# Decode attention with a large KV cache: K transposed as fp32 words, scores in two passes, and PV that streams V four tiles wide

## The chip, the cores and the metric

The kernel runs on one core of one Trainium2 chip. The metric is the device time of one execution in microseconds (us). A ratio is always the mean time of one kernel's fast runs over that of the other's fast runs of the same rounds on the same chip, so it is not quite the ratio of the medians that are quoted beside it.

The span of a profile is about 1.8 us shorter than the time of the same run; all instants below count from the span's first instruction.

## The reference

One token attends to 32,768 cached positions: 8 KV heads ("groups") with 4 query heads each, head size 128. A small SwiGLU feed-forward runs beside it, and a sigmoid gate mixes the two.

```python
def _A_ref(x, k_cache, v_cache, wq, wo):          # k_cache, v_cache: [1, 8, 32768, 128] bf16
    q = (x @ wq) as [1, 32, 1, 128]
    scores = einsum("bhqd,bhkd->bhqk", q, k) * Dh ** -0.5
    p = softmax(scores)
    o = einsum("bhqk,bhkd->bhqd", p, v)
    return o.reshape(1, 1, 4096) @ wo              # wo: [4096, 512]
# _B_ref: (silu(x @ w_gate) * (x @ w_up)) @ w_down
# result: g * a + (1 - g) * b, g = sigmoid(sum(x * gate_w))
```

K and V are 134 MB of the 148 MB that the kernel reads. Each byte is used once.

## The kernel before

One queue (SP) streams everything in a fixed order into a ring of five 4 MB slots: wq, halves of K and V (16,384 positions each), the feed-forward weights, and wo last. A slot is loaded again when PE has released it. The last half of V and wo are cut into four loads each, so that PE can follow them.

```python
RH = S // 256          # 128 tiles of 128 positions in one half
TPF = 8                # tiles per "fill"
V_LAST = (64, 32, 16, 16); WO_CUT = (16, 8, 4, 4)
stream = [("wq",), ("K", 0, 0), ("F1",), ("K", 0, 1), ("F2",)]
for g in range(1, G):
    for hf in range(2):
        stream += [("K", g, hf), ("V", g - 1, hf)]
stream += [("V", G - 1, 0), ("V", G - 1, 1), ("wo",)]
# ... SP: for each entry wait for the slot's release (five entries back), then dma_start
```

PE transposes K eight tiles at a time, DVE copies the transposed tiles out of PSUM, and PE multiplies them with the queries. ACT takes the exponential. PV uses each V tile as weights and streams four columns of probabilities through it.

```python
def emit_fill(j, src, q):
    if j >= NST:
        pe.wait_ge(sem_cp, j - NST + 1)
    stb = pst[j % NST]
    for t in range(TPF):
        ins = pe.transpose(stb[:, t * 128 : (t + 1) * 128], src[:, q * TPF + t, :], ident[:, :])
    ins.then_inc(sem_fill, 1)

def emit_scores(j):
    # ... waits
    for t in range(TPF):
        col = (q * TPF + t) * HPG
        ins = pe.matmul(ps_sc[f % NSC][:, col : col + HPG],
                        ktT[:, j % NKT, t * 128 : (t + 1) * 128],
                        qT[:, g * HPG : (g + 1) * HPG], start=True, stop=True)
    ins.then_inc(sem_sc, 1)

def emit_pv(g, hf, src, r0, n):
    for r in range(r0, r0 + n):
        k = hf * RH + r
        ins = pe.matmul(ps_o[:, g * HPG : (g + 1) * HPG], src[:, r, :], ET[:, g % NEG, :, k],
                        start=(k == 0), stop=(k == NT - 1))
    if r0 + n == RH:
        ins.then_inc(sem_pv, 1)
# ... after the last PV: DVE scales by 1/sum, transposes; PE rearranges (O2); then
for c, n in enumerate(WO_CUT):
    pe.wait_ge(sem_ldo[c], 16)
    for j in range(j0, j0 + n):
        for oc in range(OC):
            ins = pe.matmul(ps_a[:, oc, :], wo_v[:, j, oc * 128 : (oc + 1) * 128],
                            O2[:, j : j + 1], start=(j == 0), stop=(j == WOJ - 1))
    j0 += n
```

## Time and profile before

| | before |
|---|---|
| time, median of 3 | 362.18 us |
| span | 360.6 us |
| load queue, share of 16 DMA engines | 96.4% |
| PE busy; mean granted clock | 79%; 0.777 |
| 16 KB packets of the instruction queue | 51 |

The first fence is from the page. Its third part gives, for each DMA queue, packets, MB and the share of 16 engines' time; the rows of the second part have one character for each fortieth of the span, in tenths.

```profile
span 360.6 us, 14008 instructions
...
PE 283.3 (79%) x6582; PEld 277.6 (77%) x6582; DVE 187.4 (52%) x305; ACT 27.8 (8%) x140; POOL 4.2 (1%) x18
...
DMA  8999999999999999999999999999999999999972
...
q1 hardware_dynamic: 6200, 148.12, 96.4%
q8 instruction: 51, 0.84, 0.9%
...
ring<-in_A_k_cache_dram SPq DMA_DIRECT2D x16, 4096.0 KB, 36.9
...
```

The load queue is full almost throughout. The last line says that a 4 MB load lands 36.9 us after it is issued (median); at the 427 GB/s that the page gives for the middle of the span one takes about 10 us, so three or four loads are always queued. DMA therefore sets the pace, and what it carries does not depend on how PE computes. Instructions are fetched by DMA too, here in 51 packets of 16 KB (0.84 MB).

The groups of instructions (columns: line, engine, operation, output and inputs, shapes, count; busy time in us, mean ns of one; idle time ahead of them and what ended it) show the three parts that the change touches.

```profile
...
L360 PE MATMUL ps<-ident,ring 128*128 128x128 bf16 x2048 | 187.9, 252 | 21.2 <-issue 13.7
...
L375 PE MATMUL ps<-qT,ktT 128*128 128x4 bf16 x2048 | 90.9, 166 | 9.1 <-issue 7.9
...
L387 PE MATMUL ps<-ET,ring 128*128 128x4 bf16 x2048 | 64.9, 168 | 30.0 <-issue 29.6
...
```

Mean ns is the time from start to modelled end of one pipelined matmul. The pace is read from the timeline (start, duration, instructions merged, count). This is PE in the middle of the span:

```profile
...
236.20 2.77 PE L387 MATMUL ps<-ET,ring 128*128 128x4 bf16 x98 [0.58 <-issue]
...
244.23 1.01 PE L360 MATMUL ps<-ident,ring 128*128 128x128 bf16 x8
245.03 0.40 PE L375 MATMUL ps<-qT,ktT 128*128 128x4 bf16 x8
...
248.05 0.61 PE L360 MATMUL ps<-ident,ring 128*128 128x128 bf16 x8
248.50 0.34 PE L375 MATMUL ps<-qT,ktT 128*128 128x4 bf16 x8
...
```

Eight transposes take about 0.80 us when the clock is low (244.23 to 245.03, granted 0.50) and 0.45 us when it is high (248.05 to 248.50, granted 1.00), eight scores 0.2 us (248.50 to the next transposes). The 98 PV matmuls from 236.20 us are 27 ns apart, with full 128-column weights.

At the end, PE looks like this:

```profile
...
342.27 2.99 PE L387 MATMUL ps<-ET,ring 128*128 128x4 bf16 x106 [2.03 <-issue]
...
348.45 3.05 PE L387 MATMUL ps<-ET,ring 128*128 128x4 bf16 x109 [2.23 <-issue]
...
352.60 0.61 PE L456 MATMUL ps<-O,ring 128*128 128x1 bf16 x17 [0.29 <-DVE O L601]
354.71 3.26 PE L456 MATMUL ps<-O,ring 128*128 128x1 bf16 x111 [1.50 <-issue]
358.39 0.27 PE L466 MATMUL ps<-ident,res 128*4 128x128 bf16 x1 [0.43 <-DVE res L605]
```

The pauses ahead of 342.27, 348.45 and 354.71 are put down to "issue": PE waited for nothing that the profile shows. They fall in the middle of runs of matmuls that have no wait between them, after nearly equal amounts of work. The row at 352.60 is the first of wo, the last row the final small matmul before the output.

How the load traffic ends is seen in windows (each row: the window, its length, busy us of each engine, granted clock, DMA share, GB/s):

```profile
...
346.00:352.00 6.00, 3.27 (x118) 3.12 (x114) 0.48 (x3) 0.00 (x0) 0.00 (x0) 0.50 0.60 248
352.00:357.00 5.00, 3.11 (x105) 2.95 (x105) 0.24 (x2) 0.00 (x0) 0.00 (x0) 0.50 0.36 139
...
```

### The profile page before, as it was taken

The page shows a single profiled execution, that of the slowest core. Times are in us where ns is not written, and L with a number is a line of the kernel's source. Part 1 is how long each engine was busy: PE and PEld are TensorE (multiplying, and loading weights), DVE is VectorE, ACT ScalarE, POOL GpSimd, SP SyncE. Part 2 cuts the span into 40 slices and gives each one's busy share as a digit, 9 for nine tenths or more (in the row PEclk, how much of TensorE's full clock was granted, in tenths as well). Part 3 has the DMA queues.
Part 4 walks back from the last instruction along what each step waited for, and adds up shares of the span by engine and source line. Part 5 has one row for each costly group of instructions (what it writes and reads, how often), then busy time and mean ns, then how long its engine had stood idle before and what let it go on. Part 6 is the DMA issues. An engine that isn't in the chain of part 4 may idle for free.

```text
span 360.6 us, 14008 instructions
## 1 busy us (share of the span) xinstructions
PE 283.3 (79%) x6582; PEld 277.6 (77%) x6582; DVE 187.4 (52%) x305; ACT 27.8 (8%) x140; POOL 4.2 (1%) x18
## 2 busy tenths in 40 slices
PE   0439998869796897988786969889879778879674
PEld 0439997869696886988685969889779778879674
DVE  0219186637566383737384664638364744728201
ACT  1000004000110003000300012000300030000300
POOL 0000000000000000000000000000000000000000
PEclk9999678676879696778788796867895885857655
DMA  8999999999999999999999999999999999999972
GB/s 346 411 405 449 420 423 448 413 431 433 416 447 416 431 430 427 420 433 427 428 436 409 448 413 434 433 413 453 407 434 432 418 434 429 427 431 412 411 314 88
DMA packets 6260, 148.99 MB, mean 413 GB/s; under 512 B 698, under 2 KB 700, under 8 KB 1212
## 3 DMA queue, kind: packets, MB, share of 16 engines
q1 hardware_dynamic: 6200, 148.12, 96.4%
q8 instruction: 51, 0.84, 0.9%
q14 instruction: 5, 0.04, 0.0%
q10 hardware_dynamic: 4, 0.00, 0.0%
HBM read 148.11 MB, written 0.00 MB: 411 GB/s over the span
## 4 chain that ended last, share of the span: by engine, by line
PE 66%; issue 25%; DMA 6%; DVE 1%; ACT 0%; POOLq 0%; SPq 0%; POOL 0%; ACTq 0%; DVEq 0%
PE ps L360 38%; PE ps L387 13%; PE ps L375 12%; DMA ring<-in_A_k_cache_dram 6%; PE ps L332 2%; PE ps L456 1%; ACT ET L494 0%; DVE ktT L579 0%; PE ps L346 0%; DVE pmaxf L567 0%; PE ps L423 0%; POOLq L201 0%; SPq L250 0%; POOL gmax L240 0%; PE ps L466 0%
## 5 line engine op out<-in xcount | busy, mean ns | idle before, releaser
L579 DVE COPY ktT<-ps 128x1024 bf16<-128x1024 bf16 x256 | 170.7, 692 | 124.0 <-PE ps L360 123.1
L360 PE MATMUL ps<-ident,ring 128*128 128x128 bf16 x2048 | 187.9, 252 | 21.2 <-issue 13.7
L360 PEld LDWEIGHTS ps<-ident,ring 128*128 128x128 bf16 x2048 | 150.3, 114 | 24.5 <-issue 16.2
L375 PE MATMUL ps<-qT,ktT 128*128 128x4 bf16 x2048 | 90.9, 166 | 9.1 <-issue 7.9
L375 PEld LDWEIGHTS ps<-qT,ktT 128*128 128x128 bf16 x2048 | 81.5, 99 | 9.4 <-issue 8.0
L387 PE MATMUL ps<-ET,ring 128*128 128x4 bf16 x2048 | 64.9, 168 | 30.0 <-issue 29.6
L387 PEld LDWEIGHTS ps<-ET,ring 128*128 128x128 bf16 x2048 | 59.8, 101 | 31.3 <-issue 30.8
L494 ACT ACTIVATE ET<-ps,nbias 128x128 bf16<-128x128 f32 x64 | 22.5, 376 | 0.2
L484 ACT ACTIVATE nbias<-gmax 128x4 f32<-128x4 f32 x8 | 1.6, 206 | 270.3 <-POOL gmax L240 270.3
L567 DVE TENSOR_REDUCE pmaxf<-ps 128x4 f32<-128x512 f32 x16 | 11.1, 692 | 12.5 <-PE ps L375 12.5
L494 ACT ACTIVATION_READ_ACCUMULATOR ET<-ps,nbias 128x1 f32 x64 | 13.8, 216 | 0.0
L332 PE MATMUL ps<-xT,ring 128*128 128x1 bf16 x112 | 6.9, 198 | 0.0
L332 PEld LDWEIGHTS ps<-xT,ring 128*128 128x128 bf16 x112 | 6.8, 158 | 0.0
L240 POOL PARTITION_ALL_REDUCE gmax<-pmax x8 | 3.0, 373 | 321.8 <-DVE pmax L571 321.8
L301 PE MATMUL ps<-ones_bf,x_row 1*128 1x1 bf16 x4 | 0.3, 172 | 7.9 <-DMA gw_row<-in_gate_w_dram 7.9
L318 PE MATMUL ps<-xT,ring 128*128 128x1 bf16 x128 | 3.6, 165 | 3.6 <-DMA ring<-in_A_wq_dram 3.6
L318 PEld LDWEIGHTS ps<-xT,ring 128*128 128x128 bf16 x128 | 3.5, 104 | 3.6 <-issue 3.6
L301 PEld LDWEIGHTS ps<-ones_bf,x_row 1*128 1x128 bf16 x4 | 0.2, 114 | 7.9 <-DMA gw_row<-in_gate_w_dram 7.9
L456 PE MATMUL ps<-O,ring 128*128 128x1 bf16 x128 | 3.9, 165 | 1.8 <-issue 1.5
L456 PEld LDWEIGHTS ps<-O,ring 128*128 128x128 bf16 x128 | 3.6, 104 | 2.0 <-issue 1.6
L513 DVE CAST xT<-ps 128x4 bf16<-128x4 f32 x1 | 0.2, 161 | 8.4 <-PE ps L301 8.4
L605 DVE SCALAR_TENSOR_TENSOR res<-ps,g_col,b_pre 128x4 bf16<-128x4 f32 x1 | 0.2, 221 | 5.6 <-PE ps L456 5.6
(48 smaller groups left out, 16.5 us busy)
## 6 DMA issues: line engine op xcount, KB each, us to landing
ring<-in_A_k_cache_dram SPq DMA_DIRECT2D x16, 4096.0 KB, 36.9
ring<-in_A_v_cache_dram SPq DMA_DIRECT2D x15, 4096.0 KB, 33.2
ring<-in_A_wq_dram SPq DMA_DIRECT2D x1, 4096.0 KB, 12.4
ring<-in_A_v_cache_dram SPq DMA_DIRECT2D x1, 2048.0 KB, 27.9
ring<-in_A_wo_dram SPq DMA_DIRECT2D x1, 2048.0 KB, 33.7
ring<-in_B_w_gate_dram SPq DMA_DIRECT2D x1, 1792.0 KB, 26.8
ring<-in_B_w_up_dram SPq DMA_DIRECT2D x1, 1792.0 KB, 30.6
ring<-in_B_w_down_dram SPq DMA_DIRECT2D x1, 1792.0 KB, 43.5
```

What stands on the lines that cost most here:

```text
L240: pool.partition_all_reduce(gmax[:, g, :], pmax[:, g, :], 128, ReduceOp.max).then_inc(sem_gmax, 1)
L301: ins = pe.matmul(ps_m[:, base + c : base + c + 1], srcv[:, c, :], ones_bf[0:1, 0:1], start=True, stop=True,)
L318: ins = pe.matmul(ps_m[:, M_Q0 + h : M_Q0 + h + 1], wq_v[:, c, h * DH : (h + 1) * DH], xT[:, c : c + 1], start=(c == 0), stop=(c == KC - 1),)
L332: ins = pe.matmul(ps_m[:, base + j : base + j + 1], wt[:, c, :].rearrange("d (p j) -> d j p", j=FC)[:, j, :], xT[:, c : c + 1], start=(c = ...
L360: ins = pe.transpose(stb[:, t * 128 : (t + 1) * 128], src[:, q * TPF + t, :], ident[:, :])
L375: ins = pe.matmul(ps_sc[f % NSC][:, col : col + HPG], ktT[:, j % NKT, t * 128 : (t + 1) * 128], qT[:, g * HPG : (g + 1) * HPG], start=True ...
L387: ins = pe.matmul(ps_o[:, g * HPG : (g + 1) * HPG], src[:, r, :], ET[:, g % NEG, :, k], start=(k == 0), stop=(k == NT - 1),)
L456: ins = pe.matmul(ps_a[:, oc, :], wo_v[:, j, oc * 128 : (oc + 1) * 128], O2[:, j : j + 1], start=(j == 0), stop=(j == WOJ - 1),)
L484: act.activation(nbias[:, g, :], gmax[:, g, :], ACT.Copy, scale=-SCALE).then_inc(sem_nbias, 1)
L494: act.activation(ET[:, g % NEG, h, hf * RH : (hf + 1) * RH], sc[:, h, :], ACT.Exp, bias=nbias[:, g, h : h + 1], scale=SCALE, accum_out=esu ...
L567: dve.tensor_reduce(pmaxf[:, f, :], sc, AX.X, ALU.max).then_inc(sem_pmax, 1)
L579: dve.tensor_copy(ktT[:, j % NKT, :], pst[j % NST]).then_inc(sem_cp, 1)
```

## The change

The intent was to take work from PE. Two neighbouring bf16 values are moved as one fp32 word, so one transpose handles two tiles. The even and odd elements then lie interleaved, and the scores take two accumulating matmuls, each with weights that step by two elements, against queries laid out in two diagonal blocks (`qz`). For PV, the roles are exchanged: 16 columns of probabilities (4 tiles x 4 heads) are the weights, and 512 columns of V stream through. Of the 16x512 result only the four diagonal blocks are wanted; per group DVE copies it out and four fp32 matmuls with a selection matrix gather the blocks.

```diff
 def emit_fill(j, src, q):
-    stb = pst[j % NST]
-    for t in range(TPF):
-        ins = pe.transpose(stb[:, t * 128 : (t + 1) * 128], src[:, q * TPF + t, :], ident[:, :])
+    stb = pst_f[j % NST]
+    for t in range(0, TPF, 2):
+        two = src[:, q * TPF + t : q * TPF + t + 2, :].rearrange("p r d -> p (r d)")
+        ins = pe.transpose(stb[:, t * 64 : (t + 2) * 64], two.bitcast(FP32), ident_f[:, :])
 def emit_scores(j):
-    for t in range(TPF):
-        ins = pe.matmul(ps_sc[f % NSC][:, col : col + HPG], ktT[:, j % NKT, t * 128 : (t + 1) * 128],
-                        qT[:, g * HPG : (g + 1) * HPG], start=True, stop=True)
+    for t in range(0, TPF, 2):
+        kt = ktT[:, j % NKT, t * 128 : (t + 2) * 128].rearrange("p (k e) -> p e k", e=2)
+        for e in range(2):
+            ins = pe.matmul(ps_sc[f % NSC][:, col : col + 2 * HPG], kt[:, e, :], qz[:, g, e, :],
+                            start=(e == 0), stop=(e == 1))
 def emit_pv(g, hf, src, r0, n):
-    for r in range(r0, r0 + n):
-        ins = pe.matmul(ps_o[:, g * HPG : (g + 1) * HPG], src[:, r, :], ET[:, g % NEG, :, k], ...)
+    if r0 == 0 and hf == 0 and g > 0:
+        pe.wait_ge(sem_pvc, g)
+    for r in range(r0, r0 + n, TPV):                      # TPV = 4
+        ins = pe.matmul(ps_pv[0 : TPV * HPG, :],
+                        ET[:, g % NEG, k : k + TPV, :].rearrange("p r h -> p (r h)"),
+                        src[:, r : r + TPV, :].rearrange("p r d -> p (r d)"), ...)
+def emit_o(g):
+    pe.wait_ge(sem_pvc, g + 1)                            # DVE has copied ps_pv to pv_sb
+    for r in range(TPV):
+        ins = pe.matmul(ps_m[:, M_OT + g * HPG : M_OT + (g + 1) * HPG],
+                        pv_sb[:, r * DH : (r + 1) * DH], osel[0 : TPV * HPG, r, :],
+                        start=(r == 0), stop=(r == TPV - 1))
 # ... cut: ET becomes [128, NEG, NT, HPG]; set-up of ident_f, sel, qz, osel; semaphores;
 #     in the tail, emit_o(G - 2) goes before the last half's PV and emit_o(G - 1) after it
```

DVE's copies of the transposed tiles keep their size and number, and the loads and their order do not change.

More of the change, by code (lines that the diff above doesn't have):

```diff
@@ L52, in bass_gated_mix__gqa_block_cached__swiglu_ffn__decode_kernel @@
     NF = NH * FPH
+    TPV = 4
     NKT = 8
@@ L107, in bass_gated_mix__gqa_block_cached__swiglu_ffn__decode_kernel @@
         sem_qT = S_("s_qT")
+        sem_sel = S_("s_sel")
+        sem_qz0 = S_("s_qz0")
+        sem_pe_qe = S_("s_pe_qe")
+        sem_qz = S_("s_qz")
         sem_t1 = S_("s_t1")
@@ L114, in bass_gated_mix__gqa_block_cached__swiglu_ffn__decode_kernel @@
         sem_rS = S_("s_rS")
+        sem_osel = S_("s_osel")
+        sem_pvc = S_("s_pvc")
+        sem_pe_o = S_("s_pe_o")
         sem_oT1 = S_("s_oT1")
@@ L126, in bass_gated_mix__gqa_block_cached__swiglu_ffn__decode_kernel @@
         ktT = T("ktT", [128, NKT, TPF * 128], BF16)
-        ET = T("ET", [128, NEG, HPG, NT], BF16)
+        ET = T("ET", [128, NEG, NT, HPG], BF16)
         ident = T("ident", [128, 128], BF16)
@@ L145, in bass_gated_mix__gqa_block_cached__swiglu_ffn__decode_kernel @@
         qT = T("qT", [128, H], BF16)
+        ident_f = T("ident_f", [128, 128], FP32)
+        evenidx = T("evenidx", [128, 128], FP32)
+        kf1 = T("kf1", [128, 1], FP32)
+        sel = T("sel", [128, 2, 128], BF16)
+        qz = T("qz", [128, G, 2, 2 * HPG], BF16)
         sg = T("sg", [128, FC], FP32)
@@ L155, in bass_gated_mix__gqa_block_cached__swiglu_ffn__decode_kernel @@
         rS = T("rS", [128, H], FP32)
+        oidx = T("oidx", [128, TPV * HPG], FP32)
+        osel = T("osel", [128, TPV, HPG], FP32)
+        pv_sb = T("pv_sb", [TPV * HPG, TPV * DH], FP32)
         oTs = T("oTs", [128, H], BF16)
@@ L163, in bass_gated_mix__gqa_block_cached__swiglu_ffn__decode_kernel @@
         ps = es.enter_context(nc.psum_tensor("ps", [128, 8, 512], FP32))
+        pst_f = [ps[:, i, :] for i in range(NST)]
         pst = [ps[:, i, :].bitcast(BF16) for i in range(NST)]
@@ L166, in bass_gated_mix__gqa_block_cached__swiglu_ffn__decode_kernel @@
         ps_sc = [ps[:, NST + i, :] for i in range(NSC)]
-        ps_o = ps[:, 6, :]
+        ps_pv = ps[:, 6, :]
         ps_m = ps[:, 7, :]
@@ L172, in bass_gated_mix__gqa_block_cached__swiglu_ffn__decode_kernel @@
         M_Q0 = M_X0 + 2 * KC
-        M_G0 = M_Q0 + H
+        M_QE = M_Q0 + H
+        M_G0 = M_QE + 2 * H
         M_U0 = M_G0 + FC
         M_B0 = M_U0 + FC
-        M_O0 = M_B0 + OC
+        M_OT = M_B0 + OC
+        M_O0 = M_OT + H
         assert M_O0 + WOJ <= 512
@@ L223, in _ @@
                 ).then_inc(sem_ident, 1)
+                chain(pool.memset(ident_f[:, :], 0.0))
+                pool.affine_select(
+                    out=ident_f[:, :],
+                    in_=ident_f[:, :],
+                    compare_op=ALU.not_equal,
+                    fill=1.0,
+                    base=0,
+                    pattern=[[-1, 128]],
+                    channel_multiplier=1,
+                ).then_inc(sem_ident, 1)
+                pool.iota(
+                    evenidx[:, :],
+                    pattern=[[0, 2], [2, 64]],
+                    base=0,
+                    channel_multiplier=0,
+                    allow_small_or_imprecise_dtypes=True,
+                ).then_inc(sem_iota, 1)
+                pool.memset(qz[:, :, :, :], 0.0).then_inc(sem_qz0, 1)
                 pool.iota(
@@ L226, in _ @@
                     pattern=[[1, 128]],
+                    base=0,
+                    channel_multiplier=0,
+                    allow_small_or_imprecise_dtypes=True,
+                ).then_inc(sem_iota, 1)
+                pool.iota(
+                    oidx[:, :],
+                    pattern=[[HPG, TPV], [1, HPG]],
                     base=0,
@@ L310, in emit_x @@
                     pe.matmul(
-                        ps_o[:, H : H + 1], ones_f[:, :], gpart[:, :], start=True, stop=True
+                        ps_pv[:, 0:1], ones_f[:, :], gpart[:, :], start=True, stop=True
                     ).then_inc(sem_pe_g, 1)
@@ L325, in emit_q @@
                     ins.then_inc(sem_pe_q, 1)
+                    pe.wait_ge(sem_sel, 2)
+                    pe.wait_ge(sem_qT, 1)
+                    for e in range(2):
+                        ins = pe.matmul(
+                            ps_m[:, M_QE + e * H : M_QE + (e + 1) * H],
+                            sel[:, e, :],
+                            qT[:, :],
+                            start=True,
+                            stop=True,
+                        )
+                    ins.then_inc(sem_pe_qe, 1)
                 def emit_ffn():
@@ L357, in emit_fill @@
                         pe.wait_ge(sem_cp, j - NST + 1)
-                    stb = pst[j % NST]
-                    for t in range(TPF):
+                    stb = pst_f[j % NST]
+                    for t in range(0, TPF, 2):
+                        two = src[:, q * TPF + t : q * TPF + t + 2, :].rearrange(
+                            "p r d -> p (r d)"
+                        )
                         ins = pe.transpose(
-                            stb[:, t * 128 : (t + 1) * 128], src[:, q * TPF + t, :], ident[:, :]
+                            stb[:, t * 64 : (t + 2) * 64], two.bitcast(FP32), ident_f[:, :]
                         )
@@ L368, in emit_scores @@
                     if j == 0:
-                        pe.wait_ge(sem_qT, 1)
+                        pe.wait_ge(sem_qz, 4)
                     if q == 0 and f >= NSC:
@@ L372, in emit_scores @@
                     pe.wait_ge(sem_cp, j + 1)
-                    for t in range(TPF):
+                    for t in range(0, TPF, 2):
                         col = (q * TPF + t) * HPG
-                        ins = pe.matmul(
-                            ps_sc[f % NSC][:, col : col + HPG],
-                            ktT[:, j % NKT, t * 128 : (t + 1) * 128],
-                            qT[:, g * HPG : (g + 1) * HPG],
-                            start=True,
-                            stop=True,
-                        )
+                        kt = ktT[:, j % NKT, t * 128 : (t + 2) * 128].rearrange(
+                            "p (k e) -> p e k", e=2
+                        )
+                        for e in range(2):
+                            ins = pe.matmul(
+                                ps_sc[f % NSC][:, col : col + 2 * HPG],
+                                kt[:, e, :],
+                                qz[:, g, e, :],
+                                start=(e == 0),
+                                stop=(e == 1),
+                            )
                     ins.then_inc(sem_sc, 1)
                 def emit_pv(g, hf, src, r0, n):
-                    for r in range(r0, r0 + n):
+                    if r0 == 0 and hf == 0 and g > 0:
+                        pe.wait_ge(sem_pvc, g)
+                    for r in range(r0, r0 + n, TPV):
                         k = hf * RH + r
                         ins = pe.matmul(
-                            ps_o[:, g * HPG : (g + 1) * HPG],
-                            src[:, r, :],
-                            ET[:, g % NEG, :, k],
+                            ps_pv[0 : TPV * HPG, :],
+                            ET[:, g % NEG, k : k + TPV, :].rearrange("p r h -> p (r h)"),
+                            src[:, r : r + TPV, :].rearrange("p r d -> p (r d)"),
                             start=(k == 0),
-                            stop=(k == NT - 1),
+                            stop=(k == NT - TPV),
                         )
@@ L395, in emit_pv @@
                         ins.then_inc(sem_pv, 1)
+                def emit_o(g):
+                    if g == 0:
+                        pe.wait_ge(sem_osel, 1)
+                    pe.wait_ge(sem_pvc, g + 1)
+                    for r in range(TPV):
+                        ins = pe.matmul(
+                            ps_m[:, M_OT + g * HPG : M_OT + (g + 1) * HPG],
+                            pv_sb[:, r * DH : (r + 1) * DH],
+                            osel[0 : TPV * HPG, r, :],
+                            start=(r == 0),
+                            stop=(r == TPV - 1),
+                        )
+                    ins.then_inc(sem_pe_o, 1)
                 emit_x()
                 pe.wait_ge(sem_xT, 1)
-                pe.wait_ge(sem_ident, 1)
+                pe.wait_ge(sem_ident, 2)
                 scored = 0
@@ L410, in _ @@
                                 scored += 1
+                            if e[2] == 0 and e[1] >= 2 and q == LAG:
+                                emit_o(e[1] - 2)
                         continue
@@ L429, in _ @@
                         ).then_inc(sem_pe_S, 1)
+                        emit_o(G - 2)
                         r0 = 0
@@ L443, in _ @@
                     emit_pv(g, hf, src, r0, RH - r0)
+                emit_o(G - 1)
                 pe.wait_ge(sem_oT2, 1)
@@ L475, in _ @@
                 act.activation(
-                    g_col[:, :], ps_o[:, H : H + 1], ACT.Sigmoid
+                    g_col[:, :], ps_pv[:, 0:1], ACT.Sigmoid
                 ).then_inc(sem_g, 1)
@@ L494, in _ @@
                             act.activation(
-                                ET[:, g % NEG, h, hf * RH : (hf + 1) * RH],
+                                ET[:, g % NEG, hf * RH : (hf + 1) * RH, h],
                                 sc[:, h, :],
@@ L522, in _ @@
                 )
-                dve.wait_ge(sem_iota, 2)
+                dve.wait_ge(sem_iota, 4)
                 for i, thr in enumerate((32.0, 64.0, 96.0)):
@@ L539, in _ @@
                 dve.tensor_copy(pmat[:, :], pmat_f[:, :]).then_inc(sem_pm, 1)
-                dve.wait_ge(sem_pe_q, 1)
-                dve.tensor_copy(qT[:, :], ps_m[:, M_Q0 : M_Q0 + H]).then_inc(sem_qT, 1)
+                dve.tensor_scalar(
+                    osel[:, :, :].rearrange("p r h -> p (r h)"),
+                    oidx[:, :],
+                    kf[:, 0:1],
+                    None,
+                    op0=ALU.is_equal,
+                ).then_inc(sem_osel, 1)
+                dve.wait_ge(sem_pe_q, 1)
+                dchain(dve.tensor_scalar(kf1[:, :], kf[:, :], -1.0, None, op0=ALU.add))
+                for e, k in ((0, kf), (1, kf1)):
+                    dve.tensor_scalar(
+                        sel[:, e, :], evenidx[:, :], k[:, 0:1], None, op0=ALU.is_equal
+                    ).then_inc(sem_sel, 1)
+                dve.tensor_copy(qT[:, :], ps_m[:, M_Q0 : M_Q0 + H]).then_inc(sem_qT, 1)
+                dve.wait_ge(sem_pe_qe, 1)
+                dve.wait_ge(sem_qz0, 1)
+                for e in range(2):
+                    qe = ps_m[:, M_QE + e * H : M_QE + (e + 1) * H].rearrange(
+                        "p (g h) -> p g h", g=G
+                    )
+                    for b in range(2):
+                        dve.tensor_copy(
+                            qz[b * 64 : (b + 1) * 64, :, e, b * HPG : (b + 1) * HPG],
+                            qe[b * 64 : (b + 1) * 64, :, :],
+                        ).then_inc(sem_qz, 1)
                 dve.wait_ge(sem_g, 1)
@@ L573, in emit_pmax, with emit_pvc @@
                         ).then_inc(sem_pmax, 1)
+                def emit_pvc(g):
+                    dve.wait_ge(sem_pv, 2 * (g + 1))
+                    if g > 0:
+                        dve.wait_ge(sem_pe_o, g)
+                    dve.tensor_copy(pv_sb[:, :], ps_pv[0 : TPV * HPG, :]).then_inc(sem_pvc, 1)
                 for j in range(NF):
@@ L585, in _ @@
                         emit_pmax(j // FPH)
+                    if j % (2 * FPH) == 1 and j >= 4 * FPH:
+                        emit_pvc(j // (2 * FPH) - 2)
+                emit_pvc(G - 2)
                 dve.wait_ge(sem_exp, 2 * HPG * G)
@@ L593, in _ @@
                 dve.wait_ge(sem_rS, 1)
-                dve.wait_ge(sem_pv, 2 * G)
-                dve.tensor_tensor(oTs[:, :], ps_o[:, 0:H], rS[:, :], ALU.mult).then_inc(
+                emit_pvc(G - 1)
+                dve.wait_ge(sem_pe_o, G)
+                dve.tensor_tensor(oTs[:, :], ps_m[:, M_OT : M_OT + H], rS[:, :], ALU.mult).then_inc(
                     sem_oT1, 1
```

## The prediction

> **What bounds it now.** The page's queue table gives the load queue 96.4% of 16 DMA engines over the 360.6 us span, 148.1 MB; the 40 slices show DMA at 9 throughout the middle. The DMA issue list has 4 MB loads landing 33 to 37 us after issue, three and a half times the 10 us one takes, so the queue is never empty. The bytes do not change: at the mid-span 427 GB/s they are 347 us, plus some 3 us of start and 10 us of tail (1 us windows: half DMA share from 346 to 357) while PE does PV, O and wo. PE is close behind: 79% busy, 60 us idle ahead of the three big lines, almost all "issue". These pauses of 1 to 3 us come after rather regular amounts of work, and the instruction queue carries 51 packets of 16 KB. [...] I read the pauses as late refills.
>
> **What changes, per K half + V half**, for which DMA takes 20 us (steps from the timeline; cold is granted clock 0.5, warm 1.0):
> - Transposes: 128 bf16 (107 ns cold, 56 warm; 7 to 14 us) become 64 fp32. The trace's fp32 weight loads pace a pass at 213 ns cold, bf16 ones 27. [...] Estimate: 110 to 215 ns each, 7 to 14 us. No clear gain.
> - Scores: 128 before and after, weights now stepping by two. The strided FFN weights take 60 ns, unstrided 28; estimate 30 to 45, so 4 to 6 us, not 3.5.
> - PV: 128 matmuls of 28 ns (3.6 us) become 32 that stream 512 columns; scaling the transposes by four, 215 warm to 427 cold: 7 to 14 us. [...]
> - New per group: a 16x512 copy (0.7 us, as the 512-wide reduce) and four fp32 matmuls (1.7 us cold). In the tail, 2.5 us between PV and O.
> - PE instructions fall from 13,200 to about 7,500; refill pauses about halve, and 0.4 MB (1 us) less is fetched.
> - DVE's 256 copies of 692 ns stay.
>
> Sum: warm about 19 us, cold 30, against DMA's 20. [...] I expect PE at or just over DMA's pace: nothing gained in mid-span, some lost in the tail, where PV and O are critical, some won by fewer pauses. DMA forbids a large gain.
>
> **Predicted: 366 us**, 8 in 10 between 359 and 400. Faster by over 2%: 0.02; within 2%: 0.58; slower: 0.40.
>
> **Shown right by:** load queue above 94%; PE's "issue" idle well under half; PV matmuls 215 ns apart, 7 us or more per half; granted clock above 0.777; transposes 110 to 215 ns apart; the last wo load landing within 3 us of the last wo matmul. **Wrong, slow side:** DMA share under 92%, SP's waits for PV or transposes emptying the queue, K-half periods of 22 us or more.
>
> **What would make it wrong.** Transposes taking several passes (over 300 ns): PE sets the pace, 400 to 500 us. The clock staying at 0.5 through transposes or PV: 400 or more. [...] Other side: transposes at 60 ns with a warm clock give PE slack, 358 to 361 us.

The sum: it came to 19 us for a pair of halves at the high clock and 30 at the low one (with each term at its upper end nearly 35), against DMA's 20. What the cuts take is the ground for going by the 19: that PE would run mostly at the high clock was the author's estimate. So was the reading that the weight load sets the pace of an fp32 pass. The trace before shows an fp32 matmul as two records, and one such pair 212 ns apart at clock 0.5 (345.12 and 345.33 us); the 110 to 215 ns for a transpose is that pace, and half of it for the high clock. The PV estimate is four times the 56 and 107 ns of a transpose (224 and 428, put at 215 and 427).

## The result, and the profile after

| | before | after |
|---|---|---|
| time, median of 4 | 362.18 us | 359.70 us |
| ratio, 95% interval | | 0.9933 (0.9915 to 0.9950) |
| span | 360.6 us | 357.9 us |
| load queue | 96.4% | 96.9% |
| PE busy; mean clock | 79%; 0.777 | 92%; 0.967 |
| 16 KB instruction packets | 51 | 32 |

The kernel became 0.7% faster, where 1% slower had been forecast. The lines of the page that answer to those above:

```profile
span 357.9 us, 9051 instructions
...
PE 327.6 (92%) x4088; PEld 244.8 (68%) x4088; DVE 191.1 (53%) x321; ACT 28.5 (8%) x140; POOL 5.1 (1%) x23
...
DMA  8999999999999999999999999999999999999981
...
q1 hardware_dynamic: 6200, 148.12, 96.9%
q8 instruction: 32, 0.52, 0.6%
...
```

PE is busier, its clock is high nearly all the time, and 19 instruction packets fewer are fetched. The groups:

```profile
...
L418 PE MATMUL ps<-ident_f,ring 128*128 128x128 f32 x1024 | 161.8, 290 | 9.8 <-DMA ring<-in_A_k_cache_dram 9.8
...
L451 PE MATMUL ps<-ring,ET 128*16 128x512 bf16 x512 | 120.2, 379 | 0.9 <-DVE pv_sb L684 0.9
...
L437 PE MATMUL ps<-qz,ktT 128*128 128x8 bf16 x2048 | 88.4, 167 | 0.4 <-DVE ktT L690 0.4
...
```

The idle time of PE put down to "issue" is gone from these lines. The middle of the span:

```profile
...
244.37 0.64 PE L418 MATMUL ps<-ident_f,ring 128*128 128x128 f32 x4
244.84 0.34 PE L437 MATMUL ps<-qz,ktT 128*128 128x8 bf16 x8
...
247.56 5.78 PE L451 MATMUL ps<-ring,ET 128*16 128x512 bf16 x26
253.88 2.10 PE L418 MATMUL ps<-ident_f,ring 128*128 128x128 f32 x16 [0.55 <-DMA ring<-in_A_k_cache_dram]
255.82 0.34 PE L437 MATMUL ps<-qz,ktT 128*128 128x8 bf16 x8
...
```

Sixteen fp32 transposes take 1.94 us at the high clock (253.88 to 255.82, 121 ns each), four between scores 0.47 us, eight scores 0.2 us as before, and 26 PV matmuls 5.78 us, which is 222 ns each. The waits now name a load. The end:

```profile
...
341.77 7.07 PE L451 MATMUL ps<-ring,ET 128*16 128x512 bf16 x32
349.67 1.05 PE L466 MATMUL ps<-osel,pv_sb 16*128 16x4 f32 x8 [0.82 <-DVE pv_sb L684]
...
351.72 3.57 PE L538 MATMUL ps<-O,ring 128*128 128x1 bf16 x128 [0.28 <-DVE O L716]
355.72 0.27 PE L548 MATMUL ps<-ident,res 128*4 128x128 bf16 x1 [0.42 <-DVE res L720]
```

```profile
...
346.00:352.00 6.00, 4.36 (x33) 2.33 (x31) 1.27 (x4) 0.00 (x0) 0.00 (x0) 0.95 0.56 232
352.00:357.00 5.00, 3.56 (x125) 3.29 (x122) 0.50 (x2) 0.00 (x0) 0.00 (x0) 0.50 0.02 7
...
```

PE has no pauses of "issue" left, but PV of the last half alone takes 7.07 us, and O is ready at 351.7 us, hardly sooner than before (352.6). What moved is the end of the loads: in the last window DMA moved 7 GB/s instead of 139.

That can be seen engine by engine. The kernel waits until a load has added 16 to its semaphore, and the trace has 16 records of this for each load. I read each record as the landing of one DMA engine's part; the trace counts 16 engines but does not name the engine of a record, so "engine" in what follows is this reading. For the last wo load, in us:

```text
before: 346.2 346.3 346.4 346.5 347.6 347.9 348.5 352.0 355.4 355.4 355.5 355.6 355.7 355.8 357.0 357.3
after:  346.2 346.4 346.5 346.6 347.4 347.5 348.0 350.9 352.0 352.3 352.3 352.4 352.4 352.6 352.7 352.9
```

The fastest engines finish at the same instant in both. The slow half finishes 3 to 4.4 us earlier after the change. The last wo matmul waits for the last of the 16, so this is where the time may have come from; PE's own pauses before the change end at about the same instant, and the experiments have to tell the two apart. The typical load packet did not change: the median packet of 32 KB took 1.215 us in both kernels. But of the 56 packets (after the first 15 us) that took over 1.4 us before, 52 overlap in time with an instruction packet, where chance would give 41%; after the change there are 39, of which 35 overlap (chance: 26%). More closely, 46 of the 51 instruction packets before, and 29 of the 32 after, are followed by such a long load packet that starts within 0.02 us of their end. That is what two packets in line on one engine would show, though the trace does not name the engine.

From this came the theory for the experiments, called the **fetch theory**: the engines that carry loads also fetch PE's instructions; each fetch makes one of them late; lateness adds up over the whole span because the load queue never runs empty; and the kernel waits for the slowest engine. **Rival 1**: the pauses of PE in the tail cost the time, and the landing is beside the point. **Rival 2**: PE's own reading of SBUF slows the loads, and the change altered that traffic.

### The profile page after: what moved, and what is told of

The parts are those of the page before. It is cut to its first block, busy times and chain, and to the rows that moved or that the text cites. A ratio compares the mean times of both kernels' runs of the same rounds, so it can differ in the third digit from the quotient of the medians.

```text
span 357.9 us, 9051 instructions
## 1 busy us (share of the span) xinstructions
PE 327.6 (92%) x4088; PEld 244.8 (68%) x4088; DVE 191.1 (53%) x321; ACT 28.5 (8%) x140; POOL 5.1 (1%) x23
## 3 DMA queue, kind: packets, MB, share of 16 engines
q1 hardware_dynamic: 6200, 148.12, 96.9%
## 4 chain that ended last, share of the span: by engine, by line
PE 56%; DMA 40%; DVE 2%; issue 1%; SPq 0%; DVEq 0%
DMA ring<-in_A_k_cache_dram 40%; PE ps L418 23%; PE ps L451 20%; PE ps L437 8%; PE ps L387 2%; PE ps L466 1%; PE ps L538 1%; DVE pv_sb L684 1%; DVE ktT L690 1%; PE ps L401 0%; SPq L294 0%; PE ps L503 0%; PE ps L548 0%; DVE row L729 0%; DVE res L720 0%
## 5 line engine op out<-in xcount | busy, mean ns | idle before, releaser
L418 PE MATMUL ps<-ident_f,ring 128*128 128x128 f32 x1024 | 161.8, 290 | 9.8 <-DMA ring<-in_A_k_cache_dram 9.8
L418 PEld LDWEIGHTS ps<-ident_f,ring 128*128 128x128 f32 x1024 | 113.6, 145 | 18.0 <-DMA ring<-in_A_k_cache_dram 14.7
L451 PE MATMUL ps<-ring,ET 128*16 128x512 bf16 x512 | 120.2, 379 | 0.9 <-DVE pv_sb L684 0.9
L437 PEld LDWEIGHTS ps<-qz,ktT 128*128 128x128 bf16 x2048 | 85.6, 97 | 21.3 <-issue 18.1
L437 PE MATMUL ps<-qz,ktT 128*128 128x8 bf16 x2048 | 88.4, 167 | 0.4 <-DVE ktT L690 0.4
L451 PEld LDWEIGHTS ps<-ring,ET 128*16 128x16 bf16 x512 | 41.3, 89 | 52.4 <-issue 1.3
L576 ACT ACTIVATION_READ_ACCUMULATOR ET<-ps,nbias 128x1 f32 x64 | 18.2, 284 | 0.0
L684 DVE COPY pv_sb<-ps 16x512 f32<-16x512 f32 x8 | 5.4, 671 | 12.5 <-PE ps L451 12.5
L466 PE MATMUL ps<-osel,pv_sb 16*128 16x4 f32 x64 | 8.4, 250 | 3.0 <-DVE pv_sb L684 3.0
L466 PEld LDWEIGHTS ps<-osel,pv_sb 16*128 16x128 f32 x64 | 7.7, 186 | 4.0 <-DVE pv_sb L684 3.5
```

What stands on the lines that cost most here:

```text
L418: ins = pe.transpose(stb[:, t * 64 : (t + 2) * 64], two.bitcast(FP32), ident_f[:, :])
L437: ins = pe.matmul(ps_sc[f % NSC][:, col : col + 2 * HPG], kt[:, e, :], qz[:, g, e, :], start=(e == 0), stop=(e == 1),)
L451: ins = pe.matmul(ps_pv[0 : TPV * HPG, :], ET[:, g % NEG, k : k + TPV, :].rearrange("p r h -> p (r h)"), src[:, r : r + TPV, :].rearrange( ...
L466: ins = pe.matmul(ps_m[:, M_OT + g * HPG : M_OT + (g + 1) * HPG], pv_sb[:, r * DH : (r + 1) * DH], osel[0 : TPV * HPG, r, :], start=(r == ...
L576: act.activation(ET[:, g % NEG, hf * RH : (hf + 1) * RH, h], sc[:, h, :], ACT.Exp, bias=nbias[:, g, h : h + 1], scale=SCALE, accum_out=esu ...
L684: dve.tensor_copy(pv_sb[:, :], ps_pv[0 : TPV * HPG, :]).then_inc(sem_pvc, 1)
```

## The experiments

"Summed lateness" is, for the last wo load, the sum over the 16 engines of landing minus the first engine's landing (89.9 us before, 59.5 after). Every experiment's kernel passed the comparison with the reference, including three that leave most of the attention out. The comparison is thus blind to the attention part at this tolerance, and it does not vouch for the arithmetic of the other variants.

### The loads alone, with PE nearly empty (e5_skel) and with padding (e6_skel_pad, e7_skel_pad16)

```diff
 # from the kernel before; wrong result on purpose
-    for t in range(TPF):            # fills and scores
+    for t in range(1):
-    for r in range(r0, r0 + n):     # PV
+    for r in range(r0, r0 + 1):
-    dve.tensor_copy(ktT[:, j % NKT, :], pst[j % NST])
+    dve.tensor_copy(ktT[:, j % NKT, 0:128], pst[j % NST][:, 0:128])
+    # at the start DVE clears the score banks once, so that nothing unwritten is read
```

> The kernel before with nearly all PE work on K and V taken out (one transpose, one score and one PV matmul where there were eight to 128; wrong result on purpose), the same loads in the same order: about 1,000 matmuls, 8 instruction fetches of 16 KB instead of 51. Fetch theory (each fetch makes one of the slower DMA engines 1.2 to 1.5 us late, and the last load waits for the slowest engine): the 16 engines finish the last wo load within 3 us of each other, the last near 348 us instead of 357.3, time about 353 us. Rival 1 (only the PE pauses and PE work at the end cost time; DMA would land at 357 whatever PE does): the last landing stays at 356 to 357.5, time about 361. Rival 2 (matmul traffic in SBUF slows the load packets): landing early as in the fetch theory, so this run alone does not tell these two apart; the padded twin does.

Measured: 356.39 us, ratio to before 0.984 (0.9825 to 0.9855). Eight instruction packets. Fifteen engines landed between 346.3 and 348.2 us, one at 351.1; a fetch had started at 349.7 us. Summed lateness 21.3 us. The time is some 3 us over the forecast because of that one engine, but the landing is 6.2 us earlier than before: PE's program does decide when loads with fixed bytes end. Rival 1 expected the landing at 356 to 357.5 and falls in that part. The 1.2 to 1.5 us for each fetch were an estimate made before the runs; they gave 1.6 (below).

The padding adds matmuls of one row by one column to every fill:

```diff
     stb = pst[j % NST]
+    for _ in range(22):             # 16 in e7
+        pe.matmul(ps[0:1, j % NST, 511:512], ones_bf[0:1, 0:1], ones_bf[0:1, 0:1],
+                  start=True, stop=True)
```

> The run above plus 22 matmuls of one row by one column per group of eight tiles: 5,632 matmuls that read almost nothing, 52 fetches. PE stays far from busy. Fetch theory: the last landing is back at 357 us (356 to 358.5), engines spread over 10 us again, time about 361. Rival 1 and rival 2 (traffic): as the run above, within 1 us of it.

Measured: 366.32 us (362.41 to 367.68), ratio 1.0092. The slowest engine landed at 357.3 us as forecast, but the fastest at 352.8 instead of 346: here all engines had run dry at times, so the run does not test what it was meant to. The waits (engine, line, releaser, total us, times, longest) show why:

```profile
...
PE ps L361 <- issue: 77.3, 41, 2.8
...
```

PE spent 77 us in pauses put down to "issue", which I read as refills. In all kernels looked at, two fetches started no closer than about 6 us (5.9 before, 6.0 after, 5.8 here) while all 16 engines were loading; here they came 6.5 us apart (median). After the first load PE hardly ever waited for another, so the refills set the pace. The run was inconclusive for the dispute, and was repeated with less padding:

> The stripped kernel with 16 one-by-one matmuls per group of eight tiles instead of 22, since with 22 refills at their smallest spacing of 6 us could not keep up and PE set the pace: 5,107 matmuls, 40 fetches. Fetch theory, at 1.6 us of summed engine lateness per fetch (21.3 us with 8 fetches): summed lateness 72 us (66 to 80), last landing 354.5 (353.5 to 356), time 359.5 to 361 against 356.4 without the padding. If only arithmetic, its traffic or its pauses counted: landing 348 to 351 and 356.4 as without it.

Measured: 359.61 us, ratio 0.9926 (0.9912 to 0.9939), 40 fetches, last landing 354.5 us, summed lateness 74.9 us; the first engine again at 346.2 us. All of it lies in the ranges of the fetch theory. The added matmuls read one element each, so rival 2 cannot explain 3.4 us of landing (351.1 to 354.5) or 54 us of summed lateness. The lines of the page, first without and then with the padding:

```profile
span 354.3 us, 2869 instructions
...
PE 73.1 (21%) x1011; PEld 52.9 (15%) x1011; DVE 61.4 (17%) x308; ACT 27.7 (8%) x140; POOL 4.1 (1%) x18
...
q8 instruction: 8, 0.13, 0.1%
...
```

```profile
span 357.8 us, 11061 instructions
...
PE 204.2 (57%) x5107; PEld 166.3 (46%) x5107; DVE 75.9 (21%) x308; ACT 27.8 (8%) x140; POOL 4.1 (1%) x18
...
q8 instruction: 40, 0.66, 0.7%
...
```

PE has slack in both. The padding also raises PE's busy share, but of what the DMA engines carry only the instruction queue's packets differ. (The two runs were on different chips; the kernel before took 362.21 and 362.37 us there.)

### The K side alone (e1_k_only), and its instructions padded (e4_k_only_pad, e9_k_only_twice)

```diff
 # from the changed kernel: PV in the old form; emit_o, its copies and their waits removed
-    for r in range(r0, r0 + n, TPV):
+    for r in range(r0, r0 + n):
         k = hf * RH + r
-        ins = pe.matmul(ps_pv[0 : TPV * HPG, :], ET[...16 columns], src[...512 columns], ...)
+        ins = pe.matmul(ps_pv[:, g * HPG : (g + 1) * HPG], src[:, r, :], ET[:, g % NEG, k, :], ...)
```

> The changed K side alone, PV in its old narrow form: about 5,560 matmuls, 44 fetches. Fetch theory: last landing between the two kernels, linear in fetches at 0.23 us each: 355.6 us (355 to 356.3), and the end follows it by 0.7 us unless a refill pause falls there: time 360 to 361.5. Rival 1: pauses at the end stay since PV still runs 128 matmuls per half, so 361 to 362 and the landing does not matter. If the wide PV were a loss on the critical path of 3.5 us or more in the tail and nothing else counted, this run would be at 356.

Measured: 361.01 us, ratio 0.9967 (0.9952 to 0.9982), 43 fetches, last landing 356.0 us. As the fetch theory had it; the time alone would also fit rival 1, which expected 361 to 362. The end of its PE timeline tells them apart:

```profile
...
351.15 1.85 PE L532 MATMUL ps<-O,ring 128*128 128x1 bf16 x64 [3.56 <-DMA ring<-in_A_wo_dram]
...
354.77 0.58 PE L532 MATMUL ps<-O,ring 128*128 128x1 bf16 x16 [0.25 <-DMA ring<-in_A_wo_dram]
356.00 0.59 PE L532 MATMUL ps<-O,ring 128*128 128x1 bf16 x16 [0.65 <-DMA ring<-in_A_wo_dram]
...
```

The wide form of PV is gone and PE now waits for each cut of wo; the last wo matmuls start with the landing at 356.0 us. This kernel is bound by the loads to the last wo matmul, and its tail has no pause of "issue".

> The run above plus 896 matmuls of one row by one column spread over the transposes (25 us of PE time in all, 1.6 us per pair of halves, where PE has some 5 us to spare): 50 to 51 fetches. Fetch theory: last landing later than in the run above by 1.6 us (1 to 2.5), time later by about as much. Rivals: no change beyond 0.4 us.

The edit is the padding above, three or four matmuls ahead of each fill's transposes. Measured: 451.22 us (433.21 to 456.44); three of the four executions were slow, and the profile is of the fast one, 433.21 us. PE was busy 94% and set the pace, so this run says nothing about the dispute. Two things made it slow. Where its clock was high, a padded fill with its scores took 0.91 us (189.69 to 190.60) where e1 takes 0.67 to 0.68; that is an estimated 60 us for 256 fills, where I had counted 25 ns for each added matmul, 25 us in all. And in most of the span after 184 us, where the clock record begins, the granted clock was 0.5:

```profile
...
205.97 1.12 PE L423 MATMUL ps<-ident_f,ring 128*128 128x128 f32 x4
206.88 0.40 PE L442 MATMUL ps<-qz,ktT 128*128 128x8 bf16 x8
...
```

Four fp32 transposes took 0.91 us here (205.97 to 206.88 by the next scores), as at the low clock in the changed kernel (0.88, 259.63 to 260.51), and 0.50 us where the clock was high (189.69 to 190.19). Why the clock stayed low with PE so busy is open. The test was then made with full-size matmuls, by computing half of the score pairs twice:

```diff
-    for t in range(0, TPF, 2):
+    for t in (0, 0, 2, 2, 4, 6):
```

> The changed K side with narrow PV, and half of its score pairs done twice (same result): 1,024 more matmuls, 25 to 29 us of PE time spread over all K halves where PE waits for loads anyway, 51 fetches against 43. Fetch theory: last landing 357.3 (356.8 to 358) against 356.0, time 362.2 to 363 against 361.0. If fetches did not matter: 361.0 within 0.3.

Measured: 362.30 us, ratio to before 1.0001 (0.9986 to 1.0017), 51 fetches, last landing 357.1 us, summed lateness 88.7 us. The end of its PE timeline:

```profile
...
357.19 0.58 PE L532 MATMUL ps<-O,ring 128*128 128x1 bf16 x16 [0.65 <-DMA ring<-in_A_wo_dram]
...
```

The kernel with the fp32 transposes and with as many fetches as the kernel before has the time of the kernel before, and it waits for the last landing. This adds PE work and its traffic along with the fetches; that it is the fetches follows from it together with e7.

### The PV side alone (e2_pv_only)

```diff
 # from the changed kernel: emit_fill and emit_scores as before (bf16, one pass, qT)
```

> The changed PV alone, transposes and scores as before (bf16, one pass): about 5,110 matmuls, 40 fetches. Fetch theory: last landing near 354.7 us (354 to 355.5). PE per pair of halves: 128 transposes of 56 to 107 ns, 128 scores, 32 PV of 222 ns, 18 to 24 us, so PE may set the pace if the clock stays low; if it does not, the end comes 2 to 3 us after the last landing or after PV, time 360 to 362. If the clock is low: above 365.

Measured: 362.55 us, ratio 1.0007 (0.9990 to 1.0024), 40 fetches, last landing 354.5 us. The landing is 2.8 us earlier than before, and nothing of it is left:

```profile
...
344.94 7.07 PE L444 MATMUL ps<-ring,ET 128*16 128x512 bf16 x32
352.84 1.05 PE L459 MATMUL ps<-osel,pv_sb 16*128 16x4 f32 x8 [0.82 <-DVE pv_sb L677]
...
354.91 3.57 PE L531 MATMUL ps<-O,ring 128*128 128x1 bf16 x128 [0.29 <-DVE O L709]
...
```

The wo matmuls start only at 354.91 us, after the last landing, and run for 3.57 us; PV and the gathering of O are on the critical path. The time lies 0.5 us above the 360 to 362 expected: the last wo matmul starts 3.8 us after the landing, not 2 to 3. The wide PV by itself saves fetches and gives all of that back in the tail.

### The tail of the changed kernel (e3_last_narrow, after_again, e8_hybrid)

```diff
 # e3: in the last group (g == G - 1) PV in the old form, straight into PSUM columns;
 #     no copy and no emit_o for it; oTs in two pieces
```

> The changed kernel with the last group's PV in the old narrow form (256 matmuls of 28 ns for 64 of 222 ns, its result multiplied straight from PSUM, so no 16x512 copy and no four fp32 matmuls at the end): 33 to 34 fetches. In the changed kernel the last wo load lands at 352.9 us but the last wo matmul ends at 355.3, because PV and O end late. If that lag is PE's tail: the last wo matmul moves to 0.6 us after the last landing (353.2 + 0.6), time 357.9 (357.3 to 358.6), 1.8 us under the changed kernel and 1.2% under before. If instead the lag comes from the wo load itself or from refill pauses, the time stays at 359.7.

Measured: 359.12 us, ratio 0.9915 (0.9900 to 0.9929), 33 fetches. PE now waits for the loads in the tail, but the last landing was 354.0 us, not 352.9: fifteen engines had landed by 352.6, one was 1.4 us later, and a fetch had started at 351.5 us. So the forecast of 357.9 failed by 1.2 us, for a reason that the fetch theory names: a fetch late in the last load. The next run tests it, beside the changed kernel itself on the same chip. Only the last half of V goes back to the narrow form, which also takes 176 instructions out ahead of that boundary.

```diff
 def emit_pv(g, hf, src, r0, n):
+    if (g, hf) == (G - 1, 1):
+        for r in range(r0, r0 + n):
+            ins = pe.matmul(ps_m[:, M_OT + g * HPG : M_OT + (g + 1) * HPG], src[:, r, :],
+                            ET[:, g % NEG, RH + r, :], start=False, stop=(r == RH - 1))
+        # ... sem_pv as before; return
 # emit_o(G - 1) now comes before the last half (its sum is left open, no stop flag),
 # emit_o(G - 2) before the half before it
```

> The changed kernel as it is, to have it on the same chip as the next run: 359.7 us (359.4 to 360.0), last wo load at 352.9 us (352.5 to 354.3), the last wo matmul 2 to 2.5 us after it.

> The changed kernel with only the last half of V in the narrow form: it goes on accumulating on the four fp32 matmuls' sum of the half before, so the copy and those matmuls come before the last half and not after it. 4,184 matmuls, 32.7 blocks of instructions against 33.4 in the run with the whole last group narrow, where a refill packet at 351.5 us made one engine land at 354.0 while the other 15 had landed by 352.6. If that refill was the cause: here the boundary comes some 90 matmuls later, after the last wo matmul's issue, the last landing is 352.5 to 353.0, the last wo matmul ends 0.7 us later, time 357.6 to 358.4. If the 354.0 was chance or the wo load's own: time 359.0 to 359.2 as there.

Measured: 359.70 us for the changed kernel (ratio 0.9927, last landing 352.7 us), and 357.79 us for the hybrid, ratio to before 0.9875 (0.9861 to 0.9888), last landing 352.7 us. By the medians the hybrid is 1.9 us under the changed kernel and 4.6 us under the kernel before; no other complete variant tried was faster. The end of its PE timeline, to be compared with that of the changed kernel:

```profile
...
348.27 3.02 PE L552 MATMUL ps<-O,ring 128*128 128x1 bf16 x96 [0.29 <-DVE O L730]
351.53 0.69 PE L552 MATMUL ps<-O,ring 128*128 128x1 bf16 x16 [0.24 <-DMA ring<-in_A_wo_dram]
352.77 0.59 PE L552 MATMUL ps<-O,ring 128*128 128x1 bf16 x16 [0.54 <-DMA ring<-in_A_wo_dram]
...
```

The last 16 wo matmuls start with the landing at 352.7 us. In the changed kernel they came 2.2 us after it. One detail of the expectation was off: the fetch near the end moved only to 349.5 us and not past the end; it did not make its engine the last one. That the late fetch alone cost e3 its 1.2 us is therefore supported by that run's record and not isolated.

### All runs together

| run | fetches | first / last engine of the last wo load, us | summed lateness, us | last wo matmul starts, us | time, us | ratio to before |
|---|---|---|---|---|---|---|
| before | 51 | 346.2 / 357.3 | 89.9 | 357.8 | 362.18 | |
| e9_k_only_twice | 51 | 346.1 / 357.1 | 88.7 | 357.6 | 362.30 | 1.0001 |
| e1_k_only | 43 | 346.2 / 356.0 | 77.9 | 356.4 | 361.01 | 0.9967 |
| e2_pv_only | 40 | 346.1 / 354.5 | 74.1 | 358.3 | 362.55 | 1.0007 |
| e7_skel_pad16 | 40 | 346.2 / 354.5 | 74.9 | 355.0 | 359.61 | 0.9926 |
| e3_last_narrow | 33 | 346.2 / 354.0 | 63.5 | 354.5 | 359.12 | 0.9915 |
| e8_hybrid | 33 | 346.3 / 352.7 | 60.1 | 353.2 | 357.79 | 0.9875 |
| after | 32 | 346.2 / 352.9 | 59.5 | 355.1 | 359.70 | 0.9933 |
| after_again | 32 | 346.2 / 352.7 | 58.7 | 355.1 | 359.70 | 0.9927 |
| e5_skel | 8 | 346.3 / 351.1 | 21.3 | 351.5 | 356.39 | 0.9840 |

A straight line through the ten rows gives 1.6 us of summed lateness per fetch, with no row off by more than 2.2 us. Through the nine rows with 32 or more fetches, the last landing moves by 0.23 us per fetch, with no row off by more than 0.9 us; e5, with its one late engine, lies 3.7 us above that line. The two runs in which PE set the pace and the engines ran dry are left out: e6 (52 fetches, summed lateness 29.1 us) and e4.

## Why the prediction was wrong

The forecast was 366 us, that is 1% slower; the result was 0.7% faster, at the lower edge of the stated range.

**Right.** DMA stayed the bound: the load queue had 96.9%. PV matmuls are 222 ns apart, 7.1 us a half; fp32 transposes are 117 to 121 ns apart at the high clock, inside the 110 to 215 that was estimated from the fp32 weight loads. An fp32 transpose of two tiles cost about as much as two bf16 ones (117 against 2 x 56 ns); that the weight load is what takes the time is not shown. PE's sum per pair of halves at the high clock is 16 x 0.67 us for transposes and scores, 7.1 us for PV and under 1 us for the gathering and the waits for its copy, about 18.7 us against the 19 forecast and the 20 of DMA. The clock rose to 0.967, and "issue" left PE's lines. The tail did get longer by the copy and the gathering: from the last PV to the first wo matmul it is now 2.9 us (348.84 to 351.72) instead of 1.1 (351.5 to 352.6).

**Wrong, and the step that failed.** The prediction says: "refill pauses about halve, and 0.4 MB (1 us) less is fetched". It treated a fetch as bytes, spread over 16 engines. In these runs a fetch cost 1.6 us of one engine's time: the packet itself took 1.06 us, and the load packet that it meets took about 0.5 us longer (1.71 against 1.215). The 1.6 us comes out of the packets and, independently, out of the straight line through the table. Since there is one fetch for about 256 PE instructions in every run (253 to 259 records of PE and PEld for each), no run separates a fetch from some other cost of an instruction, but the packets' 1.06 and 0.5 us leave little room for one. These delays add up through the span, unevenly: the four fastest engines landed within 0.6 us of each other in every kernel of the table, and the slow half collected most of it. The last landing, which the kernel waits for, moved by 0.23 us per fetch. For 19 fetches that is 4.4 us, as measured, and not 1. (The forecast had also counted somewhat too few instructions, 7,500; the trace has about 8,200.) This one term turns the sum round: 4.4 us earlier landing, less 1.7 us because PE's tail now ends 2.2 us after the landing instead of 0.5, is 2.7 us, the difference of the spans.

**Wrong in size.** I expected PE "at or just over DMA's pace" and a mean of 366 us for that. PE stayed just under the pace, with waits for K loads between halves. The mis-sized fetch is 3.4 of the 6.3 us between forecast and result; the rest is this allowance and the tail, which the prediction does not itemise. Scores with weights stepping by two were to cost 30 to 45 ns; they cost 25 as before. The step of two bf16 values (4 bytes) cost nothing, while the feed-forward weights with a step of 28 bytes took about 60 ns a matmul in both kernels (112 in 6.86 us).

**What each half did.** The K side gave 1.2 us with 8 fewer fetches; with those fetches put back (e9) it has the time of the kernel before. The wide PV alone gave nothing: it saved 11 fetches and put them back as tail. Together they save 19 fetches, and the shorter K work lets the wide PV start earlier, so only part of the gain is lost. The hybrid recovers that part.

**Left open.** Which engines fetch, and why four of them never fall behind, is not recorded in these traces. The pauses of PE before the change and its last landing happened to end together, so in that kernel alone the two could not be told apart. Its last 111 wo matmuls ran without a gap from 354.71 us, so an earlier landing alone would not have ended it sooner; fewer fetches took away both. e1 and e9 show that the landing suffices.

## What to carry to other kernels

When the load queue never runs empty, ask what else the DMA engines carry, and whether the kernel waits for the mean engine or for the slowest: here about 256 PE instructions cost the last load 0.23 us (from 32 fetches up) although all of them together were only 0.6% of the bytes. Then count instructions, not only PE time, and keep the tail short in PE time, because there the loads no longer hide it (1.7 us was lost that way in the changed kernel). The form that is best in the stream (few wide matmuls) and the form that is best in the tail (many short ones that follow the data) can differ, and one kernel may use both (the hybrid: 357.79 us, against 359.70).

## What else the traces show of the fetches, the clock and the fp32 transposes

- With a full load queue the fetches were not hidden in the kernel before: PE paused up to 3.2 us at a time (36 pauses put down to "issue", 51 us, on the three PE groups). Fetches came no closer than about 6 us apart while all engines were loading. From 62 us on, all 22 pauses of PE of over 1 us ended 1.25 to 1.56 us after the end of an instruction packet; in the tail the packets ended at 340.93, 347.20 and 353.21 us, and PE went on at 342.27, 348.45 and 354.71.
- What a fetch cost the loads: 1.6 us of one engine's time, 2.6 times what 16 KB cost at the 32 KB per 1.215 us of the loads, and 0.23 us on the last landing.
- Bf16 transposes with scores between them ran at the high clock (eight in 0.45 us instead of 0.80). In the changed kernel sixteen fp32 transposes, after 6 us without any matmul, ran 213 ns apart from 23.84 us; the clock record begins at 27.2 us, with 1.0, and the next four took 0.47 us.
- The pace of fp32 transposes of 128x128 words was 117 to 121 ns at the high clock (four in 0.47 us from 244.37 us, sixteen in 1.94 from 253.88) and 213 to 220 at the low one (four in 0.88 us from 259.63).
